# Front of the S4/SwiGLU kernel as a fixed list with idle products, late modulation pieces in table rooms, x loads behind the inverse matrices

## Chip, cores and metric

The kernel runs on one core of a Trainium2 chip. The metric is the device time of one execution in microseconds. The engines are named as in the profile: PE (TensorE), DVE (VectorE), ACT (ScalarE), POOL (GpSimd), and SP, whose queue issues most DMAs.

## The reference, cut to what matters

The sequence has 2048 rows of width 640, everything in float32. A condition vector gives six modulation vectors; layer norm, an S4 convolution with a kernel of 128 complex modes per channel, a gated residual, a second layer norm, a SwiGLU MLP and a second gated residual follow.

```
mod = (silu(c) @ w_mod).reshape(1, 6, 1, 640)
sa, ca, ga, sb, cb, gb = mod[:, 0..5]
h = layernorm(x) * (1 + ca) + sa
K[d, l] = Re sum_n C[d, n] * exp(dt[d] * A[d, n] * l) * dt[d] * B[d, n]
y = irfft(rfft(pad(h)) * rfft(pad(K)))[:2048] + h * Dskip
x = x + ga * y
h = layernorm(x) * (1 + cb) + sb
x = x + gb * ((silu(h @ w1) * (h @ w3)) @ w2)
```

## The kernel before

The width of 640 is cut into 40 steps of 16 channels (`NS`); 8 steps make a chunk of 128 channels, and there are five chunks. A step makes the convolution kernel of its channels. The words of the written list name the parts: `PH` phases on POOL (two integer operations), `AB`, `CO`, `SI` absolute value, cosine and sine on ACT, `PA`/`XA` and `PQ`/`XQ` the fast and the slow exponents (products on PE, exponentials on ACT, into a table `A`), `E1`, `E2`, `A1`, `A2` the products of tables on DVE, `kg` the kernel on PE, `K` its scaling on DVE, `pt`/`uk` its first transform on PE and its copy by ACT into the room `uk`. The convolution of a chunk goes on in eight groups: `st` (second transform, PE), `kc` (ACT), `T` and `Y` (DVE), `iv` (inverse, PE), `zt` (store). Tables `A` rotate through seven places: four of the pool `tz`, three of `tp`.

The kernel has three parts. The front makes what the rest needs: the modulation vectors from `w_mod` (3840 columns, in eight early pieces of 256 or 128 columns and five late ones of 384), the polar form of the parameters (`polar`, for the first chunk and then for the others), LN1 of the 16 tiles of x (`ln1_load`, `ln1_norm`), their first transform (`u_stage1`, which stores `u` to a DRAM tile `us`), and the first steps. Then rounds of four steps follow the written list `ROUND`; there each engine keeps the list's order (`keep` with `in_order[0]` set). At the end the last chunk runs out, and four MLP passes of 512 rows follow.

In the front before, only ACT keeps the program's order (`act`, `acopy`); for PE, DVE, POOL and SP the framework's scheduler decides. The exponents go two steps at a time:

```
for tk in range(LAG):
    ...
    if tk % EB == EB - 2:
        exps(tk + 2); transform_k(); exps(tk + 4)
    ...
    if tk == SPC + 1:
        mod_cols(4, wm[4])
        pre.close()
        fp = ssm.enter_context(tc.tile_pool(name="fp", ...))
```

so the last modulation piece (`mod_cols(4)`) comes before the pool `fp`, from which the tiles of the convolution are taken, is opened. The two modulation lines that later steps speak of are `mod_sums` (five products of a piece, then a copy `part` by DVE) and the products with `one4` that turn it into columns. The rooms `uk[:, 1]` and `uk[:, 2]` hold modulation pieces and parameters until the convolution kernels are written into them. `x_load` brings four tiles of x (`xe`) for the last residual; its place in the program is at steps 24 to 30 of the rounds, but nothing but the pool holds its DMA back.

Of the kernel before, what the change touches and what calls it, by code (L numbers as in the profile page):

```python
# [17 lines left out]
P = 128  # L18
# [74 lines left out]
def tile_kernel(ctx: ExitStack, tc: tile.TileContext, a):  # L93
# [22 lines left out]

    def act(*args, **kw):

        return tc.keep_in_program_order(S.activation(*args, **kw))  # L119
# [26 lines left out]
    cT = kp.tile([P, KD], F32, name="cT")  # L146
    uk = kp.tile([P, 3, NA, DC], F32, name="uk")
# [18 lines left out]
    scb = pm_.tile([P, KD, NA], F32, name="scb")  # L166
# [3 lines left out]
    lt = pm_.tile([P, 2, D - DC], F32, name="lt")  # L170
    misc = pm_.tile([P, 9 * NA + 1 + P], F32, name="misc")
    selx, stepx = misc[:, :NA], misc[:, NA:4 * NA]
    s1r, c1, one4 = misc[:, 4 * NA:6 * NA], misc[:, 6 * NA:8 * NA], misc[:, 8 * NA:8 * NA + 1]
# [9 lines left out]
    def w_load(w, c0):  # L183

        n = w.shape[2]
        for i in range(c0 // 480, (c0 + n - 1) // 480 + 1):
            lo, hi = max(c0, i * 480), min(c0 + n, i * 480 + 480)
            nc.sync.dma_start(w[:, :, lo - c0:hi - c0], a["w_mod"][i][:, :, lo - i * 480:hi - i * 480])
        return w

# [23 lines left out]
    for t, n in ((misc, "misc"), (iota, "iota"), (ident, "ident")):  # L214
        nc.sync.dma_start(t, a[n])

    wm = [w_load(w, 256 * i) for i, w in enumerate(
        [w_room(1, 0, 256, 1280), w_room(1, 1, 256, 1280), w_room(1, 2, 256, 1280), w_table(), w_table()])]
# [57 lines left out]


    def mod_sums(w, pm):

        n = w.shape[2]  # L280
        for k in range(KD):
            g = slice(k % 4 * NA, k % 4 * NA + NA)
            PE.matmul(pm[g, :n], scb[:, k], w[:, k, :], start=(k < 4), stop=(k > 0), tile_position=(0, g.start))
        part = pm_.tile([P, WC], F32, name="part", bufs=2)
        V.tensor_copy(part[:, :n], pm[:, :n])
        return part

    def mod_early(i, w, tag):

        pm = psS.tile([P, 512], F32, name="pm", tag=tag, bufs=1)  # L290
        n = w.shape[2]
        part = mod_sums(w, pm)
        for b in range(n // P):
            PE.matmul(pm[:, 256 + b:257 + b], part[:, b * P:(b + 1) * P], one4, start=True, stop=True)
        V.tensor_copy(cols.rearrange("p s k -> p (s k)")[:, 2 * i:2 * i + n // P], pm[:, 256:256 + n // P])

    def mod_shift():

        sa, ca, ga, zero, inv, r, gs = (cols[:, i] for i in range(7))
# [5 lines left out]

        pr = psS.tile([P, 2, 512], F32, name="pr", tag="Z", bufs=1).rearrange("p a b -> p (a b)")
        for k in range(KD):
            PE.matmul(pr[:64, k * P:(k + 1) * P], r[:, k:k + 1].broadcast_to([P, 64]), ident, start=True, stop=True)
        V.tensor_copy(rrow[:64], pr[:64, :D])
        rc = pm_.tile([P, WC], F32, name="part", bufs=2)[:, :KD * 2 * NA].rearrange("p (k c) -> p k c", k=KD)  # L310
        V.tensor_tensor(rc, bc(c1, 1, KD), bc(r, 2, 2 * NA), op=OP.mult)
        ps = psS.tile([P, 512], F32, name="ps", tag="pk", bufs=1)
# [6 lines left out]
        V.tensor_copy(shift, ps[:, :320])  # L319

    def mod_gate():

        V.tensor_tensor(cols[:, 6], cols[:, 1], cols[:, 2], op=OP.mult)
        gt = pm_.tile([P, WC], F32, name="part", bufs=2)[:, :KD * NA].rearrange("p (k g) -> p k g", k=KD)
        V.tensor_tensor(gt, bc(tog, 1, KD), bc(cols[:, 6], 2, NA), op=OP.mult)
        pg = psS.tile([P, 512], F32, name="pg", tag="pb", bufs=1)
        PE.matmul(pg[:, :KD * NA], toq, gt.rearrange("p k g -> p (k g)"), start=True, stop=True)
        V.tensor_copy(gaT, pg[:, :KD * NA])

    def mod_cols(i, w):  # L330

        pm = psS.tile([P, 2, 512], F32, name="pm", tag="Z", bufs=1)
        part = mod_sums(w, pm[:, 0])
        lo, hi = ((0, 3), (0, 3), (0, 3), (0, 1), (2, 3))[i]
        for b in range(lo, hi):
# [791 lines left out]
```

## Time and profile before

| | us |
|---|---|
| median of 3 runs | 1021.8 (1018.88 to 1024.08) |
| profiled execution, its own time | 1021.68 |
| its span, first to last instruction | 1019.8 |

| engine | busy us | share of the span |
|---|---|---|
| PE | 954.9 | 94% |
| DVE | 604.8 | 59% |
| ACT | 513.1 | 50% |
| POOL | 254.3 | 25% |

A busy PE is not PE at its peak: an instruction is longer when the granted clock is lower, and the busy time of a pipelined matmul reaches to its modelled end. The granted clock has a mean of 0.953 over the span. In the views, a time in front is the start from the span's start, then follow the duration, engine, line of the code, output and inputs; brackets at the end hold the idle time before and what ended it.

### The profile page before, as it was taken

The page shows a single profiled execution, that of the slowest core. Times are in us where ns is not written, and L with a number is a line of the kernel's source. Part 1 is how long each engine was busy: PE and PEld are TensorE (multiplying, and loading weights), DVE is VectorE, ACT ScalarE, POOL GpSimd, SP SyncE. Part 2 cuts the span into 40 slices and gives each one's busy share as a digit, 9 for nine tenths or more (in the row PEclk, how much of TensorE's full clock was granted, in tenths as well). Part 3 has the DMA queues.
Part 4 walks back from the last instruction along what each step waited for, and adds up shares of the span by engine and source line. Part 5 has one row for each costly group of instructions (what it writes and reads, how often), then busy time and mean ns, then how long its engine had stood idle before and what let it go on. Part 6 is the DMA issues. An engine that isn't in the chain of part 4 may idle for free.

```text
span 1019.8 us, 20376 instructions
## 1 busy us (share of the span) xinstructions
PE 954.9 (94%) x8360; PEld 714.8 (70%) x8360; DVE 604.8 (59%) x1022; ACT 513.1 (50%) x699; POOL 254.3 (25%) x214
## 2 busy tenths in 40 slices
PE   5898797899899889899999999999999999999997
PEld 2544464666666666677788877788777788788886
DVE  4588966888888886664434555433645444533333
ACT  3658674999999954343234433334333344333321
POOL 1543332454454611221121111111111111111110
PEclk9955777999999999999999999999999999999999
DMA  9463495465555689686443454433533333433311
GB/s 273 154 229 121 179 212 178 127 166 134 142 148 151 177 209 269 203 228 158 120 117 98 134 178 136 123 98 95 179 96 102 91 91 93 148 95 99 96 39 52
DMA packets 107041, 146.31 MB, mean 143 GB/s; under 512 B 20836, under 2 KB 62948, under 8 KB 106948
## 3 DMA queue, kind: packets, MB, share of 16 engines
q1 hardware_dynamic: 104500, 140.09, 47.4%
q0 software_dynamic: 1024, 2.49, 0.9%
q10 hardware_dynamic: 1424, 2.43, 0.8%
q8 instruction: 66, 1.08, 0.4%
q14 instruction: 27, 0.22, 0.1%
HBM read 118.76 MB, written 26.21 MB: 142 GB/s over the span
## 4 chain that ended last, share of the span: by engine, by line
PE 71%; ACT 14%; DVE 7%; DMA 3%; POOL 2%; issue 2%; SPq 0%; DVEq 0%; ACTq 0%; POOLq 0%
PE acc L979 18%; PE pg L965 6%; PE pg L966 6%; PE pg L967 6%; PE pu L966 6%; PE pu L965 6%; PE pu L967 6%; ACT cs L119 3%; PE p L554 3%; ACT A L119 3%; ACT ph L119 3%; PE pa L416 2%; ACT L119 2%; PE pq L428 2%; PE pu L390 2%
## 5 line engine op out<-in xcount | busy, mean ns | idle before, releaser
L998 POOL TENSOR_TENSOR w<-w,gbr 128x512 f32<-128x512 f32 x55 | 83.6, 1520 | 399.6 <-DMA w<-in_w_dram 374.7
L456 POOL TENSOR_TENSOR ph<-thi,iota 128x1024 int32<-128x1024 int32 x40 | 85.4, 2136 | 176.7 <-DVE A L492 80.4
L965 PE MATMUL pg<-xh,gh 128*128 128x512 f32 x275 | 110.0, 400 | 0.1
L950 ACT CAST gh<-wg 128x640 fp32r<-128x640 f32 x55 | 40.2, 731 | 135.5 <-PE pg L966 129.2
L967 PE MATMUL pg<-xh,gl 128*128 128x512 f32 x275 | 107.5, 391 | 0.0
L966 PE MATMUL pg<-xl,gh 128*128 128x512 f32 x275 | 107.1, 389 | 0.0
L951 DVE TENSOR_TENSOR gl<-wg,gh 128x640 fp32r<-128x640 f32 x55 | 52.1, 948 | 89.4 <-ACT gh L950 86.5
L951 DVE TENSOR_TENSOR wl<-w,wh 128x640 fp32r<-128x640 f32 x55 | 47.7, 867 | 88.2 <-ACT wh L950 88.1
L965 PE MATMUL pu<-xh,uh 128*128 128x512 f32 x255 | 99.2, 389 | 0.0
L966 PE MATMUL pu<-xl,uh 128*128 128x512 f32 x255 | 99.2, 389 | 0.0
L967 PE MATMUL pu<-xh,ul 128*128 128x512 f32 x255 | 99.2, 389 | 0.0
L1023 DVE TENSOR_TENSOR hf<-pu,sg 128x512 f32<-128x512 f32 x52 | 36.0, 691 | 100.9 <-PE pu L967 100.9
L554 PE MATMUL p<-uk,s 128*64 128x256 f32 x640 | 79.3, 390 | 13.3 <-PE pa L416 5.6
L950 ACT CAST uh<-wu 128x640 fp32r<-128x640 f32 x51 | 37.3, 731 | 106.7 <-issue 67.8
L979 PE MATMUL acc<-wh,hh 128*128 128x512 f32 x224 | 87.6, 391 | 0.0
L979 PE MATMUL acc<-wl,hh 128*128 128x512 f32 x224 | 87.3, 390 | 0.0
L950 ACT CAST wh<-w 128x640 fp32r<-128x640 f32 x55 | 40.0, 727 | 91.1 <-PE acc L979 91.1
L979 PE MATMUL acc<-wh,hl 128*128 128x512 f32 x208 | 80.9, 389 | 0.0
L554 PEld LDWEIGHTS p<-uk,s 128*64 128x64 f32 x640 | 45.3, 138 | 39.0 <-PE pa L416 8.4
L965 PEld LDWEIGHTS pg<-xh,gh 128*128 128x128 f32 x275 | 51.6, 188 | 17.6 <-issue 5.6
L967 PEld LDWEIGHTS pg<-xh,gl 128*128 128x128 f32 x275 | 51.6, 188 | 11.3
L966 PEld LDWEIGHTS pg<-xl,gh 128*128 128x128 f32 x275 | 51.7, 188 | 10.1
(218 smaller groups left out, 2073.4 us busy)
## 6 DMA issues: line engine op xcount, KB each, us to landing
wg<-in_wg_dram SPq DMA_DIRECT2D x55, 320.0 KB
wu<-in_wu_dram SPq DMA_DIRECT2D x51, 320.0 KB
w<-in_w_dram SPq DMA_DIRECT2D x51, 320.0 KB
us<-u SPq DMA_DIRECT2D x16, 640.0 KB
s<-in_s_dram SPq DMA_DIRECT2D x40, 256.0 KB
i<-in_i_dram SPq DMA_DIRECT2D x40, 256.0 KB
uk<-us SPq DMA_DIRECT2D x32, 256.0 KB
zs<-zt SPq DMA_DIRECT2D x32, 256.0 KB
```

The costliest lines, as they stand in the source:

```text
L119: return tc.keep_in_program_order(S.activation(*args, **kw))
L390: PE.matmul(pu[h][hh * 64:hh * 64 + 64, q, :320], s1r[r], x[r, hh * 320:hh * 320 + 320], start=not (one and h == 0), stop=True, tile_posit ...
L456: hold(G.tensor_tensor(p, bc(thi[:, sl], 2, NPH), bc(iota, 1, SD), op=OP.mult))
L554: keep(PE.matmul(p2[par * 64:par * 64 + 64, pi, c, :], s2[:, pi * 2 + par, c * 64:c * 64 + 64], uk[:, 0:kn + 1:kn, f, :], start=True, stop ...
L950: S.copy(hi, src)
L951: V.tensor_tensor(lo, src, hi.bitcast(F32), op=OP.subtract)
L965: PE.matmul(ps, wh, xh, start=(i == 0), stop=False)
L966: PE.matmul(ps, wh, xl, start=False, stop=False)
L967: PE.matmul(ps, wl, xh, start=False, stop=(i == n - 1))
L979: PE.matmul(acc[k], lhs, rhs, start=(f == 0 and i == 0), stop=(f == NFT - 1 and i == len(terms) - 1))
L998: G.tensor_tensor(w2r[:, :512], w2r[:, :512], gbr, op=OP.mult)
L1023: V.tensor_tensor(hf, pu, sg, op=OP.mult)
```

## The change

The whole front, from the end of the first polar form to the state in which the round begins whose first product of tables is that of step 14, is a list of 568 words, `FRONT`; PE, DVE, POOL and the DMAs that SP issues keep its order as well. Of the words, 72 are `wm`: the last digit of their number says how many idle products (128x128 by 128x512, of a part of `lml` cleared by DVE) PE does there, 139 in all, into the bank `pk`. Ahead of the list 25, 10 and 5 more stand. The modulation is cut into sixteen pieces; pieces 8 to 10 are loaded into tables `A` and summed in the bank `A`, pieces 11 to 15 into `uk[:, 2]`. The parts of LN1, `u_stage1`, the modulation and the second polar form become words of their own. Each of the 16 tiles of x, the pieces and the parameters are loaded where the list says. The copy `scb` goes: `sc` is broadcast in the product. The x loads `xe` are issued after the last load of an inverse matrix (`i1`). The rounds, the end and the MLP are as they were; words that the front has done are skipped.

```
     V, G, PE = InOrder(nc.vector), InOrder(nc.gpsimd), InOrder(nc.tensor)   # each call through keep()
+    def load(out, in_):
+        ins = nc.sync.dma_start(out, in_)
+        return tc.keep_in_program_order(ins) if sp_order[0] else ins
...
+    ROOMS = [(1, 0), (1, 1), (1, 2), None, None, (1, 0), (1, 1), (1, 2), None, None, None, (2, 0), (2, 1), (2, 2), (2, 0), (2, 1)]
+    TAGS = "pb pk pb pk pb pk pb pk A A A Z Z Z Z Z".split()
+    PIECES = [(256 * i, 256) for i in range(7)] + [(1792, 128)] + [(1920 + 256 * i, 256) for i in range(7)] + [(3712, 128)]
...
-            PE.matmul(pm[g, :n], scb[:, k], w[:, k, :], ...)
+            PE.matmul(pm[g, :n], sc[:, k:k + 1].broadcast_to([P, NA]), w[:, k, :], ...)
...
-        pu = [psS.tile([P, 2, 512], F32, name="pu", tag=t, bufs=1) for t in ("Z", "AB"[j % 2])]
+        pu = puq[j] = [psS.tile([P, 2, 512], F32, name="pu", tag=t, bufs=1) for t in "ZA"]
...
-            pA[s] = psS.tile([P, 2, 512], F32, name="pa", tag="AB"[s % 2] if not in_order[0] else "B", bufs=1)
+            pA[s] = psS.tile([P, 2, 512], F32, name="pa", tag="B", bufs=1)
...
-        if g % 2 == 0:
+        if ch not in Zq or ch == NDC - 1 and g % 2 == 0:
             Zq[ch] = psS.tile([P, 2, 4, DC], F32, name="pz", tag="Z", bufs=1)
...
     def x_load(j):
         xe.append(fp.tile([P, D], F32, name=f"xe{j}", bufs=1))
-        nc.sync.dma_start(xe[j], a["x"][j * P:(j + 1) * P, :])
+        with tc.issue_after(i1_last[0].ins):
+            nc.sync.dma_start(xe[j], a["x"][j * P:(j + 1) * P, :])
...
+    parts.update({"ms": mod_sums, "mp": mod_part, "mc": mod_cols, "mv": mod_vec, "lb": ln1_stats, "lr": ln1_dev,
+                  "ls": ln1_mean, "ln": ln1_norm, "up": u_stage1, "ue": u_evict0, "ud": u_evict1, "us": u_store,
+                  "lw": mod_load, "lx": ln1_load, "lq": mod_load, "lg": lambda k: mod_load(5 + k),
+                  "ul": lambda k: u_load(0, k), "wm": lambda k: warm(k % 10)})
...
+    def warm(n, tag="pk"):
+        ps = psS.tile([P, 512] if tag == "pk" else [P, 2, 512], F32, name="ps", tag=tag, bufs=1)
+        ps = ps if tag == "pk" else ps[:, 0]
+        x = lml[:, 1:].rearrange("p k n -> p (k n)")
+        for _ in range(n):
+            PE.matmul(ps, x[:, :P], x, start=True, stop=True)
...
+    WARM = (25, 10, 5)
+    for word in "lw+0 lw+1 lw+3 lw+4 lw+2".split(): ...
+    V.memset(lml[:, 1:].bitcast(F32), 0.0)
+    warm(WARM[0], "Z")
...
+    do("ms", 0)
+    warm(WARM[1], "Z")
...
-    for tk in range(LAG):
-        ...
+    FRONT = (
+        "PH+1 mp+1 PA+0 PH+0 mc+1 mv+1 mc+0 wm+2 lx+1 XA+0 PQ+1 wm+12 mv+0 AB+0 lx+2 ms+2 lx+0 XQ+1 mp+2 wm+25 lb+1 "
+        "PH+2 mc+2 lp+0 PH+3 wm+33 CO+0 lx+3 PQ+0 mv+2 wm+42 lb+2 ms+3 ms+4 lb+0 mp+3 mp+4 mc+3 lr+0 XQ+0 ls+0 mv+3 "
+        "PA+1 ln+1 wm+52 AB+1 mc+4 XA+1 wm+61 CO+1 up+1 wm+78 E1+0 mv+4 lx+4 sh+0 v1+0 sc+0 lx+5 lb+5 sp+0 g1+0 sd+0 "
+        "PA+3 lg+1 ue+1 wm+83 ud+1 lb+3 XA+3 lb+4 ln+0 lr+1 lg+0 lg+2 lq+8 SI+1 lx+7 sr+0 SI+0 lx+6 wm+99 ls+1 E1+1 "
+        "sv+0 lr+2 g2+0 E2+1 ln+2 wm+104 AB+2 up+0 a1+0 wm+111 v4+0 PA+4 ms+5 A1+1 mp+5 ud+0 ms+6 ue+0 E2+0 ln+3 up+2 "
+        "mc+5 A2+1 mp+6 XA+4 lc+0 mv+5 us+1 ue+2 A1+0 PA+2 ud+2 ms+7 us+0 lx+8 ls+2 XA+2 mp+7 mc+7 mc+6 A2+0 mv+7 "
+        "wm+121 lb+6 up+3 wm+131 mv+6 PQ+3 ln+5 CO+2 wm+141 lb+8 gs+0 gp+0 AB+3 ud+3 lx+11 ue+3 ln+4 up+4 XQ+3 wm+152 "
+        "PH+5 PH+4 lx+9 us+2 AB+5 PQ+2 XQ+2 wm+161 ga+0 lb+7 ud+4 kg+0 lb+9 E1+2 PQ+6 E2+2 ms+8 K+0 ue+4 CO+3 SI+2 "
+        "wm+171 mp+8 SI+3 pt+0 v2+0 kg+1 lx+10 CO+5 XQ+6 A1+2 lr+3 PQ+5 uk+0 ls+3 us+3 AB+4 XQ+5 ln+6 A2+2 K+1 SI+5 "
+        "wm+183 PA+5 lq+9 wm+192 E1+3 CO+4 SI+4 v3+0 mc+8 wm+203 pt+1 wm+216 E2+3 lr+4 uk+1 ls+4 mv+8 kg+2 up+5 XA+5 "
+        "A1+3 A2+3 K+2 ue+5 PA+7 wm+221 kg+3 PH+6 ln+7 ud+5 ln+9 us+4 K+3 lq+10 XA+7 E1+5 up+6 wm+235 a3+0 us+5 ud+6 "
+        "a2+0 E2+5 v7+0 PQ+4 wm+241 ms+9 lx+14 wm+253 PH+8 ue+6 mp+9 mc+9 wm+262 lb+10 AB+6 mv+9 XQ+4 CO+6 lb+11 "
+        "ms+10 wm+273 mp+10 lr+5 mc+10 wm+281 AB+8 A1+5 mv+10 PA+6 wm+291 E1+4 up+7 A2+5 ud+7 ue+7 g3+0 us+6 wm+301 "
+        "pt+2 ln+8 v5+0 lx+15 ls+5 us+7 XA+6 wm+312 up+8 A1+4 wm+322 ue+8 PQ+7 E2+4 kg+5 ud+8 uk+2 up+9 pt+3 XQ+7 "
+        "lb+14 PH+7 lq+11 K+5 ud+9 ue+9 CO+8 wm+332 SI+6 AB+7 pT+0 ln+11 a4+0 A2+4 E1+6 PH+11 lb+15 lr+7 kg+4 lx+12 "
+        "ms+11 K+4 mp+11 v6+0 wm+343 CO+7 uk+3 us+9 E2+6 SI+8 lx+13 mc+11 A1+6 SI+7 wm+351 ls+7 PQ+8 us+8 wm+363 "
+        "lq+13 mv+11 pt+5 XQ+8 ln+10 lq+12 E1+7 AB+11 A2+6 wm+371 lq+14 PA+12 A1+7 wm+381 uk+5 XA+12 up+10 kg+6 lb+12 "
+        "ud+10 PQ+9 ue+10 K+6 lb+13 XQ+9 ln+14 up+11 wm+391 PA+8 XA+8 E2+7 A2+7 lr+6 wm+401 CO+11 us+10 SI+11 ue+11 "
+        "pt+4 ud+11 PH+9 kg+7 ms+12 K+7 ls+6 wm+412 ln+12 mp+12 PQ+12 E1+8 XQ+12 wm+421 ln+13 mc+12 wm+432 mv+12 E2+8 "
+        "up+12 us+11 A1+8 wm+441 ue+12 ud+12 PA+11 wm+452 A2+8 XA+11 up+13 wm+461 ln+15 PQ+11 wm+473 us+12 ud+13 "
+        "XQ+11 PA+13 wm+481 ue+13 PH+10 up+14 AB+9 XA+13 PA+9 E1+11 uk+4 ue+14 us+13 ud+14 kg+8 XA+9 PH+12 pt+7 K+8 "
+        "wm+491 E2+11 CO+9 up+15 wm+501 uk+7 PQ+10 us+14 wm+512 ue+15 SI+9 ud+15 ms+13 A1+11 wm+521 E1+9 A2+11 us+15 "
+        "pt+6 XQ+10 A1+9 AB+12 PH+13 wm+531 PA+10 kg+11 K+11 XA+10 PQ+14 l2+11 mp+13 mc+13 uk+6 mv+13 E2+9 wm+542 "
+        "XQ+14 lq+15 l2+10 ms+14 AB+10 CO+12 wm+551 PQ+15 CO+10 mp+14 wm+561 SI+12 A2+9 pt+8 SI+10 XQ+15 wm+571 E1+12 "
+        "ul+0 mc+14 mv+14 E2+12 kg+9 K+9 st+10 wm+581 ms+15 wm+591 E1+10 kc+10 uk+8 ul+1 A1+12 mp+15 A2+12 T+10 l1+11 "
+        "l2+12 l1+12 PA+15 wm+601 PH+14 pt+9 Y+10 mc+15 AB+13 ul+2 wm+611 XA+15 kg+12 K+12 st+11 PQ+13 uk+9 A1+10 "
+        "kc+11 l2+13 E2+10 mv+15 wm+621 XQ+13 A2+10 AB+14 CO+13 PH+15 PH+16 T+11 pt+11 CO+14 wm+631 PA+14 Y+11 kg+10 "
+        "K+10 st+12 wm+642 l1+10 kc+12 iv+10 T+12 Y+12 uk+11 SI+13 E1+13 wm+651 A1+13 XA+14 iv+11 wm+661 st+13 wm+672 "
+        "E2+13 AB+15 kc+13 T+13 Y+13 pt+10 zt+11 l2+14 wm+681 ul+3 iv+12 CO+15 AB+16 wm+692 st+14 wm+701 l1+13 iv+13 "
+        "wm+711 SI+14 uk+10 A2+13 "
+    ).split()
+    in_order[0] = sp_order[0] = True
+    for word in FRONT:
+        do(*run(word))
+    sp_order[0] = False
```

More of the change, by code (lines that the diff above doesn't have):

```diff
@@ L454, in phases @@
         p = tp.tile([P, SD, NPH], I32, name="ph", bufs=4)
-        hold = tc.keep_in_program_order if 0 < s < 4 else keep
-        hold(G.tensor_tensor(p, bc(thi[:, sl], 2, NPH), bc(iota, 1, SD), op=OP.mult))
-        keep(G.tensor_tensor(p[:, :, :NA], p[:, :, :NA], bc(phi[:, sl], 2, NA), op=OP.add))
+        G.tensor_tensor(p, bc(thi[:, sl], 2, NPH), bc(iota, 1, SD), op=OP.mult)
+        G.tensor_tensor(p[:, :, :NA], p[:, :, :NA], bc(phi[:, sl], 2, NA), op=OP.add)
         ph[s] = p
```

405 lines of the change are left out of this document (232 added, 173 removed).

## The prediction

> **What bounds the kernel now.** I read the page first, for the share of each engine along the span; then the windows, to price the front against the rounds behind it; then the groups of ScalarE (ACT) by shape and the timeline at four places. The page:
>
> ```profile
> span 1019.8 us, 20376 instructions
> DVE  4588966888888886664434555433645444533333
> ACT  3658674999999954343234433334333344333321
> PEclk9955777999999999999999999999999999999999
> ```
>
> Each digit is a fortieth of the span, 25.5 us. From the eighth slice on the TensorE (PE) clock is full; in slices three to seven, 51 to 178 us, it is granted at 0.5 to 0.7. That is the front. The change touches only the front and one set of x loads. The first instruction behind the front that is not in the new list is the product for step 14:
>
> ```profile
> 196.39 1.22 DVE L481 TENSOR_TENSOR E<-A,cs 128x1024 f32<-128x1024 f32 x1
> ```
>
> From there on both kernels hold the same words in the same order on PE, DVE and ACT. So the question is at what time the new list reaches this state, which now is reached at 196.4 us. The windows (columns: stretch, its length, busy us and count on PE, PE weight loads, DVE, ACT, POOL, granted clock, DMA share, GB/s):
>
> ```profile
> 0.00:17.60 17.60, 6.78 (x35) 2.79 (x36) 10.62 (x38) 8.52 (x16) 1.97 (x5) 1.00 0.94 272
> 17.60:196.40 178.80, 156.69 (x1862) 91.12 (x1859) 129.29 (x242) 116.89 (x140) 67.47 (x57) 0.74 0.58 179
> 36.00:46.00 10.00, 9.97 (x81) 4.74 (x78) 4.23 (x12) 6.75 (x8) 5.54 (x6) 1.00 0.10 32
> 46.00:50.00 4.00, 2.00 (x14) 1.13 (x10) 2.75 (x5) 3.99 (x6) 3.92 (x4) 0.91 0.11 43
> 50.00:110.00 60.00, 53.93 (x542) 27.93 (x542) 50.55 (x92) 42.82 (x53) 23.34 (x23) 0.50 0.50 179
> 110.00:120.00 10.00, 6.76 (x182) 4.43 (x174) 8.80 (x17) 4.58 (x6) 4.51 (x4) 0.97 0.70 252
> 120.00:138.00 18.00, 16.09 (x152) 8.84 (x152) 11.84 (x18) 11.11 (x13) 7.28 (x5) 0.53 0.52 166
> 138.00:155.00 17.00, 14.05 (x294) 9.18 (x292) 13.32 (x20) 16.28 (x19) 7.15 (x4) 1.00 1.06 218
> 155.00:169.00 14.00, 11.47 (x48) 5.83 (x50) 6.47 (x11) 2.36 (x3) 2.95 (x2) 0.51 0.35 126
> 196.40:224.76 28.36, 25.57 (x500) 18.65 (x498) 24.44 (x41) 26.35 (x33) 12.98 (x8) 1.00 0.57 151
> ```
>
> The last row is one round of the written list at full clock: PE is busy 25.57/28.36 = 0.90, DVE 0.86, ACT 0.93. The same engines in the front (second row) reach DVE 129.29/178.8 = 0.72 and ACT 0.65, and PE's 0.88 is mostly a slow clock. Its 178.8 us hold only as much DVE work as 150 us at the round's density. No single engine bounds the front: it is loosely packed, by a cold PE and by waits. The largest hole:
>
> ```profile
> 159.64 1.06 ACT L119 ACTIVATE cs<-ph 128x1024 f32<-128x1024 int32 x1
> 160.46 2.77 PE L283 MATMUL pm<-uk,scb 128*32 128x384 f32 x10 [1.35 <-DVE gbr L342]
> 165.87 3.33 PE L554 MATMUL p<-uk,s 128*64 128x256 f32 x16
> 169.25 0.59 ACT L122 COPY kc<-p 128x512 f32<-128x512 f32 x1 [8.56 <-PE p L554]
> ```
>
> The last modulation piece must be done before the pools of the transform open; ACT stands 8.56 us behind it, at half clock. The list spreads those pieces over the front, so this hole goes.
>
> **The change part by part.** Work that stays: each step's phases, exponentials, tables, kernel and transform, LN1, u, polar. So 129.29 us of DVE remain to within 1 us (the copy scb goes, a clearing of lml comes, pieces of 384 become pieces of 256). POOL keeps its 67.47.
>
> ACT gains. In the list's order ACT changes between Exp, Sin, Ln and Arctan 28 times after 17.6 us; now it does so 9 times:
>
> ```profile
> L119 ACT ACT_TABLE_LOAD x9 | 11.5, 1283 | 0.2
> L119 ACT ACTIVATE A<-pa 128x1024 f32<-128x1024 f32 x16 | 15.8, 1022 | 18.0 <-PE pa L416 17.8
> L119 ACT ACTIVATE x<-x,rs 128x640 f32<-128x640 f32 x16 | 13.9, 915 | 10.4 <-DVE rs L365 10.4
> 187.17 0.58 ACT L119 ACTIVATE A<-pq 128x512 f32<-128x512 f32 x1
> 187.76 1.28 ACT L119 ACT_TABLE_LOAD   x1
> 189.06 1.15 ACT L119 ACTIVATE cs<-cs,hp 128x1024 f32<-128x1024 f32 x1
> ```
>
> 19 more loads of 1.283 us are 24.4 us, so ACT's work after 17.6 is 116.89 + 24.4 = 141.3 us. At the round's 0.93 this takes 152 us and ends at 169.7. In exchange ACT need not wait for whole pairs of steps: its 17.8 us of waits for the fast exponents and 10.4 for LN1 are what the loads buy. A load costs no more than its row: it starts 0.01 us after the exponential ends (187.75) and the next activation starts 1.30 us later. The Trainium skill, "ScalarE: Activation LUTs", section "What ACT_TABLE_LOAD costs", adds a drain and gives about 2.66 us for every switch; these rows show no such drain.
>
> PE changes most. Its 156.69 busy us at a mean clock of 0.74 are some 116 us of full-clock work (an estimate: busy time times clock). Added are idle products, 128x512: 25 ahead of the first piece, 10 and 5 in the first polar part, and 139 in 72 places of the list. Their duration is that of the same shape in the MLP, 15 in 3.40 us or 0.227 us each:
>
> ```profile
> 450.67 3.40 PE acc L979 x15
> 9.89 1.88 PE L283 MATMUL pm<-uk,scb 128*32 128x256 f32 x10 [9.89 <-DMA uk<-in_w_mod_dram]
> 12.40 0.48 PE L267 MATMUL pT<-ident,lt 128*128 128x128 f32 x1 [0.62 <-DVE lt L261]
> 15.84 1.94 POOL L456 TENSOR_TENSOR ph<-thi,iota 128x1024 int32<-128x1024 int32 x1 [15.39 <-DVE thi L255]
> 18.18 0.21 DVE L275 TENSOR_SCALAR phi<-uk 128x128 int32<-128x128 f32 x1
> 18.54 1.05 POOL L457 TENSOR_TENSOR ph<-ph,phi 128x512 int32<-128x512 int32 x1 [0.76 <-DVE phi L275]
> 25.18 1.02 ACT L119 ACTIVATE A<-pa 128x1024 f32<-128x1024 f32 x1 [9.18 <-PE pa L416]
> ```
>
> The 25 take 5.7 us inside PE's 9.89 us wait for its first piece: nothing, or 0.8 us beyond that wait if they run at half clock (10.7 us). The 10 stand ahead of the first transposes: the piece ends at 11.8, the products 2.3 us later, so the transposes start 1.7 us late; at half clock 4 us. They lead to the first exponential, and that has slack until 22.5, as follows: nothing. The 139 and the last 15 together are 154 x 0.227 = 35 us. PE then has 116 + 35 = 151 us. With no gaps at all it ends at 17.6 + 151 = 168.6; at the round's 0.90, 17.6 + 167.4 = 185.0. The idle products stand where gaps are expected, so part of the round's tenth is already filled; but they are in order, and where a gap is not there they delay what follows. I take the middle, 176.8. Their place is the bank of the kernel tables (pk), so a product also waits for DVE's two operations on the previous table; the next table needs that anyway.
>
> At the start, two things. The first exponentials no longer stand behind five modulation pieces: 25.18 becomes about 18. But the list puts the phases of step 1, then step 0, ahead of the absolute phase of step 0, and ACT, in order, has the second exponential behind that: phi at 18.4, three POOL operations of 1.05, 1.94 and 1.05 us, so 22.5. Only one exponential, 1.02 us, covers 17.6 to 22.5: 3.9 us lost, which no density above contains. Front: 176.8 + 3.9 = 180.7 us.
>
> DMA is no bound: 179 GB/s over 178.8 us are 32.0 MB; over 163 us that is 196 GB/s, and the first row runs at 272. But SP's queue is now in the list's order too, so a store of u that waits for its eviction holds the modulation piece behind it, and pieces 11 to 14 are issued only some 20 to 30 words ahead of their products. Bounds: 0, or one piece's transfer late at each of the seven late pieces, 0.64 MB at 272 GB/s = 2.4 us, 17 us in all. I take 0, since the piece has 5.7 us or more (20 of 568 words in 163 us).
>
> x loads. Four of 320 KB now leave as soon as the pools open:
>
> ```profile
> 169.62 1.85 SPq L661 DMA_DIRECT2D xe<-in_x_dram  x4
> L671 PE MATMUL py<-A,i x64: 376/388/400, 403.1 to 414.1; 64*32 64x256 f32 x64
> ```
>
> They move to the rounds that make steps 24 to 31, behind loads of the inverse matrices; DMA is 0.57 busy in a round and the first reader comes at 403, so nothing. Without that cover a load behind one waits 1.2 us, four times 5 us. Early z loads on POOL, four tiles, come behind its last phases, and their tables are freed a few steps later; 403.1 covers these too.
>
> The sum, against the profiled execution's 1021.68 us (span 1019.8 and 1.9 around it; the median of the runs shown is 1021.8): 196.4 - 180.7 = 15.7 us saved, so 1006.0. Its own bounds: PE without gaps, 1021.7 - 27.8 = 994, and late pieces up to the 17 us, of which I let 10 count, 1016.
>
> **The rivals.** *The clock stays low* (slower). The mechanism: idle products of one to five at a time do not keep PE at full clock, and then they and the real work behind them last twice as long. For it: from 50 to 110 us PE is busy 53.93 of 60 us and stays at 0.50, so being busy by the records was not enough. Against it: the round runs at 1.00 with no idle product, and the drop came in 46:50, where PE was busy only half. 92 of the 178.8 us are now cold, 0.51. With that share, 151 us of work need 151/(1 - 0.51/2) = 203 us without gaps, so a front of 220 and 1046; at density 0.90, 243 and 1068. It decides from the point where 151/(1 - c/2) exceeds 178.8, c = 0.31, or less with gaps.
> The Trainium skill, "TensorE: Matmul & The Clock Gate", section "Part 1: The HAM clock gate", has about 3.4 us of sustained work restore full clock, and one idle window of that length take it. The drop fits; the restoring does not, since this trace has 60 us at 0.50, and that is why this rival keeps a chance.
>
> *The table loads come on top* (slower). If ACT's density stays at today's 0.65, 141.3 us take 217 us: front at 235, 1060. If only the loads add and nothing else is gained, 1021.7 + 24.4 = 1046. For it: 0.65 is what is measured where these words run. Against: half of that idle time is waits for PE at half clock and the hole at 160.
> A switch at double price belongs here: 19 loads twice, and 9 old ones once more, make 116.89 + 48.8 + 11.5 = 177 us, at 0.93 191 us, front at 208, 1034.
> The skill's 2.66 us a switch would give nearly this; the row at 189.06 speaks against it.
>
> *The gain is eaten by waits in line* (no change). Five in-order queues: one late transfer holds all words behind it. 17 us at late pieces bring 1006 to 1023.
>
> **How the numbers follow.** About 0.5%, 5.1 us, is what a measurement can tell from no change. Forecast, with all of 994 to 1016: 0.70, since three sums from rows (ACT 169.7, DVE 17.6 + 129.29/0.86 = 168, PE 168.6 to 185) lie below 191. Waits in line, 1017 to 1026: 0.12. Clock: 0.11. Table loads: 0.07, of it the double price 0.02. So faster 0.70, same 0.12, slower 0.18. The range reaches from 990 (PE without gaps, the clock-scaled 116 too high by 4) to 1026; the two slower cases, 0.18, are left out. The likeliest case alone: 994 to 1016.
>
> **What would show it.** Right: the product for step 14 at 175 to 187 us; clock 0.95 or more in slices one to seven; 28 loads of 1.28 us on ACT after 17.6; no hole of 8 us; rounds of 28.36 us. Wrong: a clock of 0.5 through 50 to 110 with the idle products lasting 0.43 us apart; or ACT idle more than 30 us after 22; or PE waiting for DMA at the pieces from the ninth on; or a first round that starts early and a later part that gives time back.

## The result, and the profile after

The changed kernel takes 1032.16 us (median of 5 runs, 1031.29 to 1033.75), the kernel before 1021.8 on the same chip (1018.88 to 1026.81). The ratio is 1.0087, 95% interval 1.0065 to 1.0109: slower by 9 us (by this ratio) to 10 us (between the medians), where 15.7 us less were forecast. The profiled execution took 1031.83 us; these are the lines of its page that answer to those of before:

```profile
span 1030.0 us, 20825 instructions
...
DVE  4879867578888886674444454444555544634332
ACT  4778868689999973253334433234333344433321
...
PEclk8969869999999999999999999999999999999999
```

The clock in slices three to seven is no longer 0.5 to 0.7 but 0.6 to 0.9, and ACT, which has the added table loads, is busier there. Yet the front is not shorter. The product for step 14, which ends it, and the product for step 18, one round later, in the timeline of the changed kernel:

```profile
198.26 1.22 DVE L125 TENSOR_TENSOR E<-A,cs 128x1024 f32<-128x1024 f32 x1
...
235.72 1.22 DVE L125 TENSOR_TENSOR E<-A,cs 128x1024 f32<-128x1024 f32 x1
```

and the latter in the kernel before:

```profile
224.81 1.22 DVE L481 TENSOR_TENSOR E<-A,cs 128x1024 f32<-128x1024 f32 x1
```

The first product `acc` of the MLP, in the kernel before and in the changed one:

```profile
450.51 0.39 PE L979 MATMUL acc<-hl,wh 128*128 128x512 f32 x1
```

```profile
463.07 0.39 PE L125 MATMUL acc<-hl,wh 128*128 128x512 f32 x1
```

So the front lost 198.26 - 196.39 = 1.9 us instead of winning 15.7, and the first round took 37.46 us instead of 28.4: 9.0 us more. From there `acc` is 227.35 us away (before 225.7), and the end another 566.9 (before 569.3): +1.7 and -2.4. The sum, 1.9 + 9.0 + 1.7 - 2.4, is the 10.2 us between the two spans. The windows of the changed kernel (columns as in the prediction) show front, its middle, and first round:

```profile
17.60:198.26 180.66, 167.07 (x2012) 100.75 (x2013) 139.94 (x248) 140.03 (x156) 70.82 (x57) 0.85 0.50 157
50.00:110.00 60.00, 52.95 (x692) 31.18 (x691) 53.22 (x90) 51.21 (x57) 22.84 (x20) 0.83 0.40 134
198.26:235.72 37.46, 30.81 (x524) 21.48 (x525) 24.95 (x42) 29.16 (x36) 12.97 (x8) 0.95 0.68 179
```

PE is busy 167.07 of 180.66 us, 0.92: the front is now as full of PE work as a round, and that work holds the idle products. In the first round all engines have a smaller busy share than in a round before; something is late there. The timeline at the hand-over from the list to the round, SP's issues and what waits for them (the bracket gives the idle time before an instruction and what ended it):

```profile
194.91 1.26 SPq L131 DMA_DIRECT2D uk<-us  x2
...
196.44 1.13 SPq L765 DMA_DIRECT2D zs<-zt  x2
...
197.62 0.74 SPq L131 DMA_DIRECT2D s<-in_s_dram  x1
198.41 1.63 SPq L131 DMA_DIRECT2D uk<-us  x2
...
202.94 2.81 PE L125 MATMUL p<-uk,s 128*64 128x256 f32 x16 [4.20 <-DMA s<-in_s_dram]
...
205.78 0.59 ACT L139 COPY kc<-p 128x512 f32<-128x512 f32 x1 [4.55 <-PE p L125]
206.40 0.69 DVE L125 TENSOR_TENSOR T<-p,kc 128x512 f32<-128x512 f32 x1 [6.92 <-ACT kc L139]
```

The load of the matrix for group `st+14` (tile `s`) stands in the list behind the loads of u that `st+13` issues and that must wait for it; the z store, which waits for ACT, got in between too. So it is issued at 197.62 and lands 5.2 us later, and PE, ACT and DVE wait for it one behind another. The group before it and this group on PE, `st+13` and `st+14`, in the kernel before, and `st+13` in the changed one:

```profile
186.97 1.95 PE L554 MATMUL p<-uk,s 128*64 128x256 f32 x16
...
193.09 1.95 PE L554 MATMUL p<-uk,s 128*64 128x256 f32 x16 [1.03 <-issue]
```

```profile
192.92 1.95 PE L125 MATMUL p<-uk,s 128*64 128x256 f32 x16
```

Before, `st+14` waited for no transfer. And PE is already 5.95 us late at `st+13`, where DVE's product for step 14 is only 1.9 us late: the start of step 14 makes the front look better than it is, and a part of what the first round loses was lost on PE ahead of it. That gave two places to look at: the idle products in the front, and SP's order at its end.

### The profile page after: what moved, and what is told of

Its sections match the earlier page's. It is cut to its first block, busy times and chain, and to the rows that moved or that the text cites. A ratio compares the mean times of both kernels' runs of the same rounds, so it can differ in the third digit from the quotient of the medians.

```text
span 1030.0 us, 20825 instructions
## 1 busy us (share of the span) xinstructions
PE 977.6 (95%) x8569; PEld 734.6 (71%) x8569; DVE 618.0 (60%) x1027; ACT 539.1 (52%) x718; POOL 257.5 (25%) x214
## 4 chain that ended last, share of the span: by engine, by line
PE 74%; ACT 10%; DVE 9%; DMA 4%; issue 1%; POOL 1%; SPq 0%; ACTq 0%; DVEq 0%
PE pg L125 19%; PE pu L125 18%; PE acc L125 18%; PE ps L125 5%; PE p L125 4%; ACT cs L136 2%; PE pq L125 2%; ACT A L136 2%; PE pk L125 2%; DVE uk L125 2%; ACT ph L136 2%; PE pa L125 2%; PE pt L125 2%; PE pz L125 2%; DMA zs<-zt 2%
## 5 line engine op out<-in xcount | busy, mean ns | idle before, releaser
L125 PE MATMUL pg<-xh,gh 128*128 128x512 f32 x280 | 112.2, 401 | 0.1
L125 DVE TENSOR_TENSOR E<-A,cs 128x1024 f32<-128x1024 f32 (+1 forms) x80 | 79.4, 1013 | 4.3 <-PE pk L125 2.9
L125 PE MATMUL ps<-lml 128*128 128x512 f32 x179 | 70.1, 490 | 5.8 <-DVE lml L125 4.2
```

The source lines that it names most:

```text
L125: return lambda *args, **kw: keep(fn(*args, **kw))
```

## The experiments

Below, "step 14" and "step 18" are the start times of DVE's two products shown above (before: 196.39 and 224.81), each read from the one execution that was profiled. Ratios are to the kernel before, run beside each experiment.

**Without idle products.** All `wm` words go from `FRONT`, and the three calls of `warm` ahead of it.

```
-    warm(WARM[0], "Z") ... warm(WARM[1], "Z") ... warm(WARM[2], "Z")
-    FRONT = "... mc+0 wm+2 lx+1 XA+0 PQ+1 wm+12 mv+0 ..."
+    FRONT = "... mc+0 lx+1 XA+0 PQ+1 mv+0 ..."
```

> The new list with no idle product at all: the 72 places in the list and the 25, 10 and 5 ahead of it are left out, all else as in the changed kernel (1032.2 us, front end at 207.4 us of the span). Theory A (the idle products themselves lie on PE's path: 138 of them keep PE busy for 57.7 us where 31 were reckoned): PE's own work of 114 us no longer binds, VectorE's 142 us do, the front ends near 185 and the time is 1008 to 1014. Theory B (PE is bound by its cold clock, which the idle products at least hold at 0.85 in the mean): without them the clock falls to the 0.74 of the kernel before or lower, PE's work grows to 130 us and more in longer waits, and the time stays at 1026 to 1036. Theory C (the 19 added table loads on ScalarE bind): no change, 1030 to 1033, and ScalarE near 0.76 busy as now.

(The 207.4 us in this text equals step 18 less one round of 28.36 us; the product of step 14 itself lies at 198.26.) Measured: 1027.51 us, ratio to before 1.0055 [1.0026, 1.0084]. Step 14 and step 18 in its timeline:

```profile
188.96 1.22 DVE L125 TENSOR_TENSOR E<-A,cs 128x1024 f32<-128x1024 f32 x1
...
225.88 1.22 DVE L125 TENSOR_TENSOR E<-A,cs 128x1024 f32<-128x1024 f32 x1
```

The front ends 9.3 us earlier than in the changed kernel, although the clock from 17.6 to 188 us falls from 0.84 to 0.74. The products do buy clock, but they cost the front more than the clock gives back. The first round is long here too (36.9 us): its loss is another matter. The time lies in the range of theory B, whose clock came out as well; the earlier end of the front is what speaks against it. The time fell by less than the front's end: the span of this execution, the fastest of ten, is 6.4 us shorter, and the ratio 0.0032 lower, some 3 us.

**Idle products in the first half only.** The words `wm` behind `v6+0` go; 87 products in 34 places stay.

> Idle products kept ahead of the list and in the list up to the word v6+0 (87 products in 34 places; in the trace of the changed kernel that is until 118 us), left out behind it (52 products in 38 places). In 120 to 195 us of the changed kernel PE is busy 73.4 of 75 us, so Theory A gives the whole cost of the late ones back, 38 places of 0.43 us to 0.9 us, about 20 us at the clock as granted: 1011 to 1016. Theory B: the late clock falls and eats that, 1024 to 1034. Theory C: 1030 to 1033.

Measured: 1026.36 us, 1.0042 [1.0016, 1.0069]; step 14 at 191.48, step 18 at 228.06. Of the 9.3 us, 6.8 come from the products of the second half here. This split does not hold with the loads ahead (below): there the second half costs 4.6 us, and the first half with the products ahead of the list another 4.6 (198.18, 193.62, 189.03).

**Without the table loads.** `AF.Abs` instead of `AF.Sin` in the front's cosines and sines, so that ACT hardly changes tables there (the sines are not computed).

```
-        act(sn, ph[s], AF.Sin, scale=2 * math.pi / TURN)
+        act(sn, ph[s], AF.Abs if front[0] else AF.Sin, scale=2 * math.pi / TURN)
```

> In the list the cosine and sine activations take the absolute value in place of the sine (same shapes, scale and bias; this part of the computation is changed), so ScalarE switches its tables in the front only for the logarithm and the arc tangent: some 25 loads of 1.283 us, 32 us, go. Theory C: the front shortens by 15 to 25 us, 1007 to 1017. Theories A and B: ScalarE is 0.76 busy and its loads fill its waits, so little is gained, 0 to 6 us, 1026 to 1032.

Measured: 1035.88 us, 1.0127 [1.006, 1.0193]; step 14 at 193.59, step 18 at 232.30. Some 25 loads fewer, 32 us of ACT's work, bring the end of the front forward by 4.7 us; the time, above every range expected, shows no gain. So most of the loads are hidden in the front, not all. What it gained was lost again behind it: step 18 comes 3.4 us earlier, `acc` 0.9, and the span is 2.4 us longer (1032.4). The four runs spread over 9.5 us.

**One load ahead.** The word `l2+14`, the load that PE waited for, is moved ahead of `l1+10`.

> One word is moved: the load of the second-transform matrix for group 14 goes some 20 words ahead, in front of the two stores of the first inverse result, behind which it now lands at 202.9 us (5.18 us in flight) while PE waits 4.2 us for it. Theory D (a transfer late in its queue is a part of the loss): 4 to 6 us gained, 1026 to 1028. If PE is made up for by what follows (ScalarE or VectorE late at the same place): 0 to 2 us gained, 1030 to 1032.

Measured: 1033.13 us, 1.0113 [1.0046, 1.0179]; step 14 at 196.72, step 18 at 234.84, a first round of 38.1 us. The wait for s is gone; its successor, in this kernel's timeline:

```profile
203.35 2.08 PE L125 MATMUL pz<-Y,i 64*128 64x128 f32 x16 [3.84 <-DMA i<-in_i_dram]
```

The next load in SP's line (an inverse matrix) was as late, and the time did not fall. One load of a late queue proves nothing either way; the next runs move the whole line.

**SP's order free.** One line: `load` no longer holds SP to the list.

```
-        return tc.keep_in_program_order(ins) if sp_order[0] else ins
+        return ins
```

> The changed kernel with one thing undone: SP's loads and stores are no longer held in the order of the list (the other engines are). Theory S (the loss of the changed kernel against before lies mostly in the first round after the list, because SP's fixed order brings the loads of the forward and inverse matrices late there): the round from the product of step 14 to that of step 18 shrinks from 37.5 us to 28 to 32 us, and the kernel comes to 1022 to 1027 us. Rival R (the first round is long because of something else, such as PE's or POOL's order at the end of the list): that round stays at 36 to 38 us, and the time at 1030 to 1035.

Measured: 1026.16 us, 1.0021 [1.0005, 1.0037]; step 14 at 196.37, step 18 at 227.99: a first round of 31.6 us.

**All loads ahead.** The order stays fixed, the loads stand as early as their three buffers allow:

```
-  l2+11 ... l2+10 ... ul+0 ... ul+1 ... l1+11 l2+12 l1+12 ... ul+2 ... st+11 ... l2+13 ... st+12 ... l1+10 ... l2+14 ... ul+3 ... l1+13
+  l2+11 ... l2+10 ... ul+0 ul+2 ul+3 l1+10 l1+11 l1+12 l2+12 ... st+10 ... ul+1 l2+13 ... st+11 l2+14 ... iv+11 l1+13 l1+14 l2+15 ... st+13
```

> The changed kernel with its list's last loads moved ahead and none taken out: the five loads of s2, five of i1 (one more of each than in the list), and the last two loads of u's first chunk each stand as early as their three buffers allow, ahead of the loads and the store that wait for PE. Theory S: the first round after the list takes 28 to 30 us instead of 37.5, the kernel 1022 to 1025 us. Rival R: 36 us or more, the kernel at 1030 to 1035 us.

Measured: 1026.01 us, 1.0024 [1.0, 1.0048]. Its timeline:

```profile
198.18 1.22 DVE L125 TENSOR_TENSOR E<-A,cs 128x1024 f32<-128x1024 f32 x1
...
198.58 1.95 PE L125 MATMUL p<-uk,s 128*64 128x256 f32 x16
...
229.79 1.22 DVE L125 TENSOR_TENSOR E<-A,cs 128x1024 f32<-128x1024 f32 x1
```

The same product of `st+14` starts 4.4 us earlier than in the changed kernel and waits for no transfer; the round takes 31.6 us. Two different edits of SP's order bring the same 6 us: this part of the loss is SP's order, shown twice.

**Loads ahead, idle products in the first half only.**

> The loads moved ahead as in the run above, and the idle products of the list kept only up to the middle of the list (87 of 138, those of the second half gone), which by itself took the product of step 14 from 198.3 to 191.5 us. Theory S, with the two losses adding up: the product of step 14 at 190 to 193 us, the first round at 28 to 31 us, the kernel at 1013 to 1018 us, under before. Rival R: the first round stays at 36 us and the kernel at 1025 to 1028 us. If the two losses hide each other: 1020 to 1024 us.

Measured: 1020.8 us, 0.9982 [0.9961, 1.0004]; step 14 at 193.62, step 18 at 224.31, a round of 30.7 us. The time misses the range of theory S by 3 us and lies in that of the losses that hide each other: the front ended 2 us later than without the loads' move. The run without any idle products, two below, decides: they add up. (The profiled execution, 1025.85 us, is one of the slowest of ten, 1016.62 to 1026.07; its stretch from step 18 to `acc`, 231.6 us, is 4 us longer than in the two runs above, so its trace is read up to step 18 alone.)

**x loads as before.** `issue_after` is taken out of `x_load`.

> The changed kernel with its third part undone: the four x loads no longer wait behind the loads of the inverse matrices. They lie in the third and fourth rounds, so theory S says: the same as the changed kernel within 2 us (1030 to 1034 us), the first round unchanged at 37.5 us. Rival X (the x loads' place costs or brings time at the hand-over to the part after the rounds): the distance from the last round's end to the first product of the part behind it changes from 80.9 us towards before's 79.3, and the time by 2 to 5 us.

Measured: 1033.33 us, 1.0101 [1.0045, 1.0156]; step 14 at 199.53, first round 36.9 us, and 226.6 us from step 18 to `acc` (227.35 in the changed kernel). The x loads' place costs or brings nothing that can be seen.

**Loads ahead, no idle products.**

> Loads moved ahead as in the two runs with that edit, and every idle product gone, those ahead of the list too. Without the products, but with the late loads, the product of step 14 was at 189.0 us and that of step 18 at 225.9; with the loads ahead and half the products, at 193.6 and 224.3. If the two losses add up (the loads' some 6 us, the products' some 7): step 14 at 189 to 191, step 18 at 218 to 221 us, the kernel at 1014 to 1018 us, under before. If the products earn as much as they cost once the loads are in time: step 18 at 223 to 226 us and the kernel at 1020 to 1023 us.

Measured: 1017.44 us (1016.28 to 1018.58), 0.9945 [0.9927, 0.9963]. All three numbers lie where the losses add up. This version beats both kernels: the list of the change, without idle products, with its loads ahead. Step 14 and step 18, and the windows of its front and first round:

```profile
189.03 1.22 DVE L125 TENSOR_TENSOR E<-A,cs 128x1024 f32<-128x1024 f32 x1
...
219.72 1.22 DVE L125 TENSOR_TENSOR E<-A,cs 128x1024 f32<-128x1024 f32 x1
```

```profile
17.60:189.03 171.43, 144.15 (x1880) 90.60 (x1882) 139.55 (x248) 139.62 (x156) 71.61 (x57) 0.78 0.57 175
189.03:219.72 30.69, 27.68 (x519) 20.09 (x516) 24.60 (x41) 28.67 (x36) 12.97 (x8) 1.00 0.61 170
```

Against the same kernel with all idle products (198.18, 1026.01 us), the front ends 9.2 us earlier, as it did without the loads' move. It still ends 8.3 us later than the forecast 180.7. Which engine holds it? PE is busy 0.84 of the time, DVE and ACT 0.81. Four of the next five runs cut work or a way from this kernel; one tries shorter idle products. A difference of 1 or 2 us in step 14 is not told from chance: each is one execution, and where fronts differ only in the order of their loads, step 14 lay at 188.96 and 189.03, at 191.48 and 193.62, and at 196.37 to 199.53.

**Less DVE.** The row statistics read half of the columns (the other half is left out of mean and variance):

```
-            V.bn_stats(lnst[p][:, i, h, :], xt[j][:, h * 320:h * 320 + 320])
+            V.bn_stats(lnst[p][:, i, h, :], xt[j][:, h * 320:h * 320 + 160])
```

> The kernel of the run above, and the 32 row statistics on DVE over 160 columns instead of 320 (half of the columns are left out of mean and variance): 32 x 0.477 us = 15.3 us of DVE become about 8, all before 126 us of the span. If DVE sets the pace of the front up to there, the product of step 14 comes 4 to 7 us earlier than in the run above and the kernel with it; if PE at its low clock sets it, it comes 0 to 2 us earlier.

Measured: 1015.18 us, 0.9924 [0.9896, 0.9951]. Step 14 at 187.86, 1.2 us earlier for 32 x (0.477 - 0.310) = 5.3 us of DVE:

```profile
187.86 1.22 DVE L125 TENSOR_TENSOR E<-A,cs 128x1024 f32<-128x1024 f32 x1
```

PE's clock from 17.6 to 188 us was 0.74 here and 0.78 in the run above, which blurs the comparison.

**Short idle products.** Loads ahead and all idle products, each over 128 columns.

> Loads moved ahead, and all 178 idle products kept at their places, each over 128 columns instead of 512. With 512 columns the product of step 14 came at 198.2 us, without idle products at 189.0. If the products' length on PE is the cost (0.23 us each in a group) and each place's own 0.2 us is small beside it: step 14 at 190 to 193 us, the kernel at 1018 to 1021. If the places cost (71 waits in PE's order, each for the one idle tile): 195 to 198 us and 1023 to 1026. If short products keep the clock up as well as long ones, it shows in the list's mean clock, 0.85 with the long ones and 0.75 without any.

Measured: 1027.25 us, 1.0055 [1.0027, 1.0083]. That is above both ranges. Its profiled execution is the fastest of ten (1022.89), so its step 14, 192.26, says little of the median; the time is that of the long products (1026.01) or above. Its clock and the products' durations are plain, in its window and in the answer for the tile of the idle products:

```profile
17.60:188.00 170.40, 156.92 (x1974) 106.42 (x1976) 134.40 (x240) 135.31 (x152) 71.68 (x57) 0.74 0.55 170
```

```profile
L125 PE MATMUL ps<-lml x179: 271/415/478, 1.7 to 195.1; 128*128 128x128 f32 x179
```

A quarter of the columns, but a median of 0.415 us by the records, partly at a low clock, and a clock of 0.74, no higher than without any (0.74 and 0.78). All executions agree: the mean clock of the whole span is 0.955 here over ten runs, 0.951 and 0.958 in the two kernels without idle products over ten and six, and 0.971 with the long ones over ten. So short products buy next to no clock and do not make the kernel faster than the long ones do. That speaks for the places, the waits in PE's order, as a part of the cost; length and clock changed together, so the run does not separate them.

**u without its way through memory.** The loads of the first chunk's u read x (that chunk's u is left out of the result):

```
+                                      a["x"].rearrange("(f b) d -> b f d", b=64)[:, fs, lo:hi] if ch == 0 else
                                       usr[h, c, :, fs, lo - h * 320:hi - h * 320])
```

> No idle products, loads moved ahead, and the eight loads of the first chunk's u take their bytes from x instead of from u, so that they wait for no store of u (the first chunk's u is left out of the result). In the chain of the run without idle products the last store of u, SP's issues behind it and the load back hold 154.1 to 167.4 us. If this way through memory is the bound that the front meets once the idle products are gone: the product of step 14 comes 4 to 9 us earlier than 189.0, the kernel at 1009 to 1014 us. If PE is as late anyway: 0 to 2 us earlier, 1015 to 1018 us.

Measured: 1017.95 us, 0.9959 [0.9929, 0.9989]; the 13 us that this way holds in the chain are gone, and the next chain is as late:

```profile
188.43 1.22 DVE L125 TENSOR_TENSOR E<-A,cs 128x1024 f32<-128x1024 f32 x1
```

**Less PE.** In steps 0 to 14 the exponents leave out the products with the low halves `lal` and `lml`:

```
-        for w, st in ((lah, True), (lal, False)):
+        for w, st in (((lah, True),) if steps[0] < 15 else ((lah, True), (lal, False))):
```

> The kernel without idle products and with the loads ahead, and in the exponents of steps 0 to 14 the products with the low halves are left out (part of the precision of these steps is not computed): 2 of 4 and 4 of 8 products a step, 15/16 of the 20.2 us that these groups take in that kernel's list, some 19 us of PE at the clock it had. If PE at its low clock sets the pace of the list: the product of step 14 comes 5 to 12 us earlier than 189.0 and the kernel at 1006 to 1012 us. If PE and DVE hand the bound to each other: 1 to 4 us earlier, 1013 to 1017 us.

Measured: 1015.13 us, 0.9925 [0.9895, 0.9954]; step 14 only 0.8 us earlier:

```profile
188.25 1.22 DVE L125 TENSOR_TENSOR E<-A,cs 128x1024 f32<-128x1024 f32 x1
```

The cut was smaller than expected: the 19 us are a sum over groups whose records overlap, and in the window from 17.6 to 188 us PE was busy 139.51 us instead of 143.42, 3.9 us less (at a clock of 0.81 instead of 0.78). So this run does not rule out that PE sets the pace. The windows without the cut and with it:

```profile
17.60:188.00 170.40, 143.42 (x1874) 90.09 (x1876) 138.52 (x245) 138.60 (x155) 71.61 (x57) 0.78 0.57 175
```

```profile
17.60:188.00 170.40, 139.51 (x1788) 84.57 (x1790) 139.85 (x250) 139.28 (x156) 71.85 (x57) 0.81 0.58 177
```

**Less PE and less DVE.** Both cuts.

> Both cuts: the low halves of the exponents left out on PE, and the row statistics over half of the columns on DVE, which by itself brought 1.2 us. If PE alone sets the pace: as the run above within 2 us. If PE and DVE hand the bound to each other, more than both alone: the product of step 14 5 to 10 us earlier than 189.0.

Measured: 1013.95 us, 0.9907 [0.9872, 0.9942]. Step 14, and two lines of the chain of waits ahead of it (start, duration, what):

```profile
183.16 1.22 DVE L125 TENSOR_TENSOR E<-A,cs 128x1024 f32<-128x1024 f32 x1
```

```profile
148.70 3.44 DMA us<-u
...
154.24 8.71 DMA uk<-us
```

5.9 us earlier, where the single cuts gave 1.2 and 0.8. That would fit PE and DVE handing the bound to each other, with u's way through memory as the chain once both are lighter; it rests on one execution of each kernel, and the times do not show it. By the ratios the single cuts brought 2.1 and 2.0 us, each inside its interval, and both together 3.9: no more than their sum. Of the 5.9 us this execution, the slowest of four, kept 1.5 of span (1015.2 and 1013.7): 3.3 us are given back between step 18 and the MLP's product `acc`, and 1.1 behind it. The same stretch was 4 us longer in one execution above too; why was not tried.

## Why the prediction was wrong, point by point

The forecast of 1006.0 us fell short by 26 us. The front, put at 180.7, ended at 198.26 by step 14: 17.6 us. Of these, 9.2 go when the idle products go; the other 8.3 stay without them, and what holds them is open. The round, taken as unchanged at 28.36, took 37.46: 9.1 us, of which 5.9 are SP's order. Behind the round the two kernels differ by less than 1 us. So two steps failed: PE at full clock with idle products that pay for themselves, and SP's fixed order at nothing.

*"From there on both kernels hold the same words in the same order."* False for SP, and this was 6 of the 10 us. The words on PE, DVE and ACT are the same, but the state in which they begin is not: before, SP's queue had its loads of matrices issued in time for the round (`st+14` at 193.09 waits for none); the list left them behind loads that wait for PE and a store that waits for ACT. The prediction bounded SP's fixed order at the modulation pieces, 0 to 17 us, and took 0; it never asked what SP still owed at the hand-over. Its own list of signs had "a first round that starts early and a later part that gives time back"; the round gave time back, though it had not even started early. The rest of the first round, from 31.6 to 28.4 us, is ACT's and PE's state at the hand-over (30.7 without idle products): with the loads ahead PE reaches `st+14` at 198.58, 5.5 us later than before, and step 18 is 5.0 us late. It was not taken apart further.

*PE: 151 us of full-clock work, at full clock.* The work is about right: 167.07 busy us x 0.85 are 142 us. The clock is not: 0.85, and 0.83 in 50 to 110 us, where 1.00 was taken. At full clock and the same busy share, 0.92, these 142 us would take 154 (an estimate, if nothing else held the list), 26 less than the 180.66 of the window. This is the term that was mis-sized. The idle products alone: they raise the clock from 0.78 to 0.85 and PE's work from 144.15 x 0.78 = 112 to 142 us, and with the loads ahead the front ends at 198.18 with them and at 189.03 without: 9.2 us on the debit side, and some 8 us of time (ratios 1.0024 and 0.9945). That the front ends earlier without them is shown by two pairs of runs. That it is their time on PE which costs, and not their waits for the bank `pk`, is argued from the chain of waits alone, where they hold 24% from 118 to 188 us. The rival that the clock stays low had the mechanism and the sign of this term. Its point of decision was a share c = 0.31 of cold work; a mean clock of 0.85 is 1 - c/2 at c = 0.30, so by its own rule the front came out at the edge, where nothing is won. Its price of 24 us and more (1046 and above) was too high, since it left c at 0.51.

*Idle products of 0.227 us.* True inside a row of them, not for a group that stands alone. The groups of the changed kernel's front, and three of its places, with the window around them (clock 1.00):

```profile
L125 PE MATMUL ps<-lml 128*128 128x512 f32 x135 | 56.2, 498 | 4.1 <-DVE lml L125 2.5 <-DVE K L125 0.9 <-DVE cols L125 0.6
...
L136 ACT ACT_TABLE_LOAD x28 | 35.9, 1283 | 0.5
...
L125 DVE TENSOR_TENSOR E<-A,cs 128x1024 f32<-128x1024 f32 x14 | 21.6, 1543 | 4.3 <-PE pk L125 2.9 <-ACT A L136 0.9 <-ACT cs L136 0.5
```

```profile
89.90 0.47 PE L125 MATMUL ps<-lml 128*128 128x512 f32 x1 [0.94 <-DVE K L125]
...
96.11 0.96 PE L125 MATMUL ps<-lml 128*128 128x512 f32 x3
97.94 0.71 PE L125 MATMUL ps<-lml 128*128 128x512 f32 x2
```

```profile
90.00:105.00 15.00, 14.55 (x180) 8.37 (x180) 14.12 (x27) 13.29 (x15) 7.57 (x9) 1.00 0.39 134
```

One takes 0.47, two 0.71, three 0.96: about 0.22 us for the group and 0.24 for each product. By the records 135 products of the list, in some 70 places, hold 56.2 us of PE, partly at a lower clock; 135 x 0.227 are 31. (A record reaches to its modelled end, so not all of the 56.2 us is time that the next product loses.) And one group, at 118.23, stands 2.5 us behind DVE's write of `lml`, as the row shows: the products read the part of `lml` that the second polar form fills.

*The start, 3.9 us lost.* The waits came as forecast: the first exponential at 19.32 (forecast about 18), ACT's absolute value, which the second exponential stands behind, at 22.84 (forecast 22.5), and between them a wait for POOL. What this adds to the front's end no run tells.

```profile
19.32 1.02 ACT L136 ACTIVATE A<-pa 128x1024 f32<-128x1024 f32 x1 [3.03 <-PE pa L125]
22.84 1.06 ACT L136 ACTIVATE cs<-ph 128x1024 f32<-128x1024 int32 x1 [2.50 <-POOL ph L125]
```

*ACT: 28 loads at 1.283 us, 141.3 us of work.* Right: x28 in the row above, and 140.03 us. Most of them stand in waits: without 25 of them, 32 us, the front ended 4.7 us earlier. The Trainium skill's 2.66 us a switch ("ScalarE: Activation LUTs", "What ACT_TABLE_LOAD costs") is not borne out here: in the changed kernel a load starts at 24.40 and the next activation at 25.70, 1.30 us later.

*POOL 67.47, DVE 129.29 within 1 us.* Both came out higher: POOL 70.82, DVE 139.94 in the same part of the kernel. Some 4 us of DVE's 10.7 are in the product shown in the last row of the groups above, 21.6 us for 14 where before they took 17.6: the list lets phases on POOL run beside it more often. The smaller product of the same line, of 512 columns, took 1.8 us less (10.0 instead of 11.8). The rest was not taken apart. A product with phases beside it, one without, and the phases of POOL:

```profile
136.13 2.67 DVE L125 TENSOR_TENSOR E<-A,cs 128x1024 f32<-128x1024 f32 x1
...
162.59 1.22 DVE L125 TENSOR_TENSOR E<-A,cs 128x1024 f32<-128x1024 f32 x1
```

```profile
135.81 1.91 POOL L125 TENSOR_TENSOR ph<-thi,iota 128x1024 int32<-128x1024 int32 x1
137.79 1.90 POOL L125 TENSOR_TENSOR ph<-ph,phi 128x512 int32<-128x512 int32 x1
```

Three of the 14 take 2.65 us or more; before, the longest was 1.93. No run took this overlap away, so its share of the front is read from the trace, not shown. Here both get longer, DVE by 1.45 and POOL's second operation by 0.85 us, as if they took turns: DVE's product ends at 138.80, 1.22 us after 137.58, near the end of POOL's first operation (137.72), and POOL's second one ends at 139.69, 1.05 us after 138.64, near the end of DVE's. The Trainium skill ("SBUF — State Buffer", "Who interferes with whom") has a DVE instruction with two SBUF inputs contend with a GpSimd (POOL) instruction that reads SBUF, and calls the pair of ports that they share an exclusive lock; these rows agree.

*Three sums that all lie below 191, so the front is shorter.* They bounded each engine alone. A cut of 5.3 us on DVE and one of 3.9 us on PE gave about 1 us of the front each, which is within what single executions differ by; both together gave 5.9, in one execution. So which engine holds the last 8.3 us is open. A sum for each engine is a lower bound, and not a forecast, where three of them lie within 20 us of each other (168 to 185).

*The 8.56 us hole and the x loads.* The hole is gone, as said (ACT's longest wait in the list is 3.7 us), and the first exponential waits 3.03 us instead of 9.18: without the products and with the loads in time the list does end 7.4 us earlier than before, and step 18 comes 5.1 us earlier. The x loads are nothing, as said.

## What to carry to other kernels

Where an order is written out by hand up to a hand-over, compare the queues' state there too: which loads are out, which buffers are free, what waits ahead of the next load on an in-order queue. Work that is added to keep a clock up is paid on the engine that it stands on; what it buys must be measured against what it takes. When several engines have nearly the same sum, cut two of them together before saying which one bounds, and see from the busy time of a window, not from a sum of overlapping records, how much the cut took. The start of one engine's instruction is not the state of the others: here it hid 4 of the 6 us that PE was late.

## What the runs showed of the hardware that was not expected

- Clock. PE's clock does not follow its busy share: 0.50 with PE busy 0.90 of 50 to 110 us before, 0.83 with 0.88 in the changed kernel. Products of 512 columns between the kernel's small ones went with the higher clock; in the window from 17.6 to 188 us products of 128 columns at the same places went with 0.74 at 156.92 us busy. The Trainium skill ("TensorE: Matmul & The Clock Gate", "Part 1: The HAM clock gate") has full clock come back after about 3.4 us of sustained work; the 53.93 busy us of these 60 before were not sustained enough for it. Why the long products helped and the short ones did not was not taken apart. The clock also differs between kernels with the same PE work: from 17.6 to 45 us the list without idle products had 1.00 with its loads ahead and 0.79 with its late ones.
- An isolated product of 128x512 takes 0.47 us at full clock and one more behind it 0.24; one of 128x128 takes 0.27 to 0.48 by the records, some of them at a low clock.
- A DVE product of two float tiles takes 1.22 us alone and up to 2.67 us while POOL's integer operations run, whose second one then takes 1.90 us instead of 1.05; the ends fit the two engines taking turns.
